# One fixed order of SBUF rooms: where the two operands of each matmul start

## The chip, the cores and the metric

The kernel runs on 1 core of one Trainium2 chip. The metric is device time in microseconds (us) of one execution. The median of three runs of the kernel before is 893.97 us.

## What is computed

Attention with fixed masks feeds two feed-forward layers in float32. `moe` has the gate below, `moe2` has s * relu(h)^2 + b. There are 2304 tokens, 512 model columns and 2048 hidden columns.

```python
scores = np.where(masks, scale * (q @ k.T), -1e9)      # 4 batches, 8 heads, 576 positions of 64
x = softmax(scores) @ v                                # -> 2304 x 512
h = x @ w_in                                           # 512 x 2048
g = np.where(h >= 1, h, np.where(h <= -1, 0, (h + 1) ** 2 / 4))
x = g @ w_out                                          # 2048 x 512
h2 = x @ w2_in
out = (s * np.maximum(h2, 0) ** 2 + b) @ w2_out
```

## The kernel before

Every float32 operand of the two feed-forward layers is held as two parts in the type fp32r, a high part (`xh`, `gh`, plane 0 of a weight) and the rest (`xl`, `gl`, plane 1). A product of two such operands is three TensorE matmuls: high by high, high by rest, rest by high. All of them have the same size: a **standing** operand of 128 partitions by 128 columns, which is loaded into the array, and a **moving** operand of 128 partitions by 256 columns, which is streamed through it. In `nc.tensor.matmul(out, a, b)`, `a` stands and `b` moves. There are 6,696 of these products.

The tokens are cut into 18 blocks g of 256: blocks 0 to 8 belong to the first feed-forward layer (the first half of the kernel, with attention woven into it), blocks 9 to 17 to the second (the second half). The hidden columns are cut into 8 pairs p. `layer1(g, p)` (line 836) does 24 products: the weights of `w_in` stand, `xh` and `xl` move. `layer2` (line 991) does 24 in the first half: the weights of `w_out` stand, the gate's two planes in `g` move. `layer2_fast` (line 904) does 21 in the second half, a seven-product form for a two by two split. There the roles are exchanged: slices of `gh` and `gl` stand and the weights move. `PASSES` says in which order blocks and pairs come, and `LAG` = 2 puts layer 2 of a pair two pairs behind its layer 1.

Between the two, `activate` (line 851) and `combine` (line 879) make the gate and its two parts on ScalarE, VectorE and GpSimd. `w_load`, `w_high`, `w_bits` and `w_parts` bring the weights in (float64 in, two parts out).

All calls go through the recorder `Order`. It notes each operation with its operands, and `issue()` (line 272) works out a start time for each from costs and due times, sorts them, and emits them. A tile is asked of the pool only when the first operation that uses it is emitted, in `real()` (line 161). So SBUF addresses follow the order of first use. Since small tiles (`half`, `narrow`, `mx`, `sm`, `sbt`) fall between the large ones, the large ones start at different places modulo 256 bytes. All slices that a product takes of a tile lie whole multiples of 256 bytes from its start, apart from those that the change moves.

Start addresses modulo 256 of the operands, from the built program:

```text
room                              role                        before                     after
xh, xl (2 + 2 rooms)              move in layer 1             64                         64
w (32 rooms)                      stand in layer 1 and in     32 in 25 rooms, 160 in 4,  128 in all
                                  layer 2 of the first half;  128 in 2, 64 in 1
                                  move in layer2_fast
g (3 rooms)                       move in layer 2             64                         64
gh within g                       stand in layer2_fast        64                         192
gl (3 rooms: raw0, raw1, as)      stand in layer2_fast        160 in 2, 128 in 1         192 in all
```

The distance (start of what stands less start of what moves, modulo 256 bytes) over the 6,696 products is then:

```text
distance       224   96    32    64   128     0   192
before        3888 1020   883   328   266   166   145
after            0    0     0  6689     0     0     7
```

Of the kernel before, what the change touches and what calls it, by code (L numbers as in the profile page):

```python
# [20 lines left out]
P = 128  # L21
# [5 lines left out]
NF = DFF // P  # L27
# [89 lines left out]
    )  # L117


class Order:  # L120


# [30 lines left out]
    def bank(self, pool, choices, name, kind):  # L153


        t = self.tile(pool, [P, 512], F32, f"bank_{kind}", len(self.choices) + 1, name)
        self.choices[t.tensor.name] = choices
        self.uses[t.tensor.name] = []
        return t

    def real(self, x):

        if not isinstance(x, bass.AP) or x.tensor.name not in self.place:
            return x
        (tag, _), pool, shape, dtype, bufs, name = self.place[x.tensor.name]
        if x.tensor.name not in self.tiles:
            if self.in_psum(x):
                tag, bufs = self.taken[x.tensor.name], 1
            self.tiles[x.tensor.name] = pool.tile(shape, dtype, tag=tag, bufs=bufs, name=name)
        t = self.tiles[x.tensor.name]  # L170
        v = bass.AP(tensor=t.tensor, offset=x.offset, ap=[list(d) for d in x.ap])
        return v if x.dtype == dtype else v.bitcast(x.dtype)
# [217 lines left out]
def attention_moe_moe(ctx, tc, q, k, v, w1_in, w1_out, w2_in, w2_out, s_in, b_in, consts, out):  # L390
    nc = Order(tc.nc)
# [4 lines left out]
    ident = nc.tile(sb, [P, P], F32, "ident")  # L396
    narrow = nc.tile(sb, [P, N_CONST], BF16, "narrow")
    mask_l, mask_s, ident_b = narrow[:, :N_MASK_L], narrow[:, N_MASK_L:N_MASK_L + N_MASK_S], narrow[:, N_MASK_L + N_MASK_S:]
    sbt = nc.tile(sb, [P, 2], F32, "sbt")
# [285 lines left out]
    wc = {}  # L685
# [189 lines left out]
    def turn(i, rooms, name):  # L875
        n_room[i] += 1
        return rooms[n_room[i] % len(rooms)](name)

    def combine(g, p, u, h, gt):

        (a21, a11, a22, a12), (h21, h11, h22, h12) = [[x[:, i * P:(i + 1) * P] for i in range(4)] for x in (u, h)]
        s4 = turn(0, (main["qk"][0], main["v"][0]), f"s{g}_{p}")[:, :4 * P]
        s1, s2, s3, s4_ = [s4[:, i * P:(i + 1) * P] for i in range(4)]
        gh = gt.rearrange("p x n -> p (x n)")[:, :7 * P]
        if (g, p) == LAST:
            gl = xs[g, 1][1].rearrange("p x n -> p (x n)")[:, :7 * P]
        else:
            gl = turn(1, (*main["raw"], main["s"]), f"gl{g}_{p}")[:, :7 * P].bitcast(F32R)

        def split(x, c, eng=nc.gpsimd):  # L890
            nc.scalar.activation(out=gh[:, c], in_=x, func=AF.Copy)
            eng.tensor_tensor(out=gl[:, c], in0=x, in1=gh[:, c].bitcast(F32), op=ALU.subtract)

        nc.vector.tensor_tensor(out=s1, in0=h21, in1=a22, op=ALU.add)
        nc.vector.tensor_tensor(out=s2, in0=s1, in1=h11, op=ALU.subtract)
        nc.vector.tensor_tensor(out=s3, in0=h11, in1=a21, op=ALU.subtract)
        nc.vector.tensor_tensor(out=s4_, in0=h12, in1=s2, op=ALU.subtract)
        split(u[:, P:], slice(0, 3 * P))
        split(s4, slice(3 * P, 7 * P), nc.vector if g == LAST[0] and p >= NP - 2 else nc.gpsimd)
        gs[g, p] = gh, gl  # L900
# [48 lines left out]
    def last_two(g, p0, part):  # L949
        y, o = ys.pop(g), [turn(2, (main["qk"][1], main["v"][1]), f"o{g}_{p0}_{i}")[:, :DM] for i in range(2)]  # L950
        (c21, c22), (c11, c12), (p21, p22), (p11, p12), (m1, m6), (m2, m5), (m4, m7), (m3, _) = [
            (x[:, :HM], x[:, HM:]) for x in (*o, part[:, 0], part[:, 1], *y)
        ]
        pairs = [(p, gs.pop((g, p))) for p in (NP - 2, NP - 1)]

        def multiply(n, p, x):
            a, b = PRODUCTS[n]
            o, c, w = y[n // 2][:, n % 2 * HM:(n % 2 + 1) * HM], slice(a * P, a * P + P), wt[1, p][b]
            for i, j in ((0, 0), (0, 1), (1, 0)):
                nc.tensor.matmul(o, x[i][:, c], w[:, j], start=False, stop=p == NP - 1 and i == 1, skip_group_check=True)  # L960

        def leave(i, j, c, queue):
            r0 = (g - NBLK) * N + i * P
            queue.dma_start(out=out[r0:r0 + P, j * HM:(j + 1) * HM], in_=c)

        nc.in_line = True
        for i, n in ((0, 0), (0, 1), (0, 2), (0, 3), (1, 0), (1, 1), (1, 2), (1, 3), (0, 4), (0, 5), (1, 4), (1, 5), (0, 6), (1, 6)):
            multiply(n, *pairs[i])
        nc.in_line = False
        add = dict(op=ALU.add)  # L970
        nc.scalar.activation(out=c11, in_=m1, func=AF.Copy)
        nc.gpsimd.tensor_tensor(out=p11, in0=c11, in1=p11, **add)
        nc.vector.tensor_tensor(out=c21, in0=m6, in1=c11, **add)
        nc.gpsimd.tensor_tensor(out=p21, in0=c21, in1=p21, **add)
        nc.vector.tensor_tensor(out=c22, in0=m5, in1=c21, **add)
        nc.gpsimd.tensor_tensor(out=p22, in0=c22, in1=p22, **add)
        nc.vector.tensor_tensor(out=c11, in0=m2, in1=p11, **add)
        leave(1, 0, c11, nc.sync)
        nc.vector.tensor_tensor(out=p12, in0=c22, in1=p12, **add)
        nc.scalar.activation(out=p11, in_=m7, func=AF.Copy)  # L980
        nc.vector.tensor_tensor(out=p21, in0=m7, in1=p21, **add)
        nc.gpsimd.tensor_tensor(out=c22, in0=p11, in1=p22, **add)
        leave(0, 1, c22, nc.sync)
        nc.vector.tensor_tensor(out=c21, in0=p21, in1=m4, op=ALU.subtract)
        leave(0, 0, c21, nc.scalar)
        nc.vector.tensor_tensor(out=c12, in0=m3, in1=p12, **add)
        leave(1, 1, c12, nc.scalar)
# [36 lines left out]
    half = nc.tile(sb, [P, 1], F32, "half")  # L1024

    def room(tag, width):
# [4 lines left out]
        p=[room("qp0", 5 * P), room("qp1", S)], v=[room("v0", 9 * D), room("v1", 9 * D)],  # L1031
# [64 lines left out]
    with tc.manual_schedule():  # L1096
        nc.now = -100
        nc.sync.dma_start(out=ident, in_=consts[:, N_MASK_L + N_MASK_S:])
        wide = x_room("wide", N_CONST)[:, 0]
        nc.sync.dma_start(out=wide[:, :N_CONST], in_=consts)  # L1100
        nc.gpsimd.memset(half, 0.5)
        nc.vector.tensor_copy(narrow, wide[:, :N_CONST])

        nc.now = -1000
        zeros = nc.tile(sb, [P, 2 * N], F32R, "u", bufs=U_BUFS)
        nc.gpsimd.memset(zeros.bitcast(F32), 0.0)
        idle = nc.bank(ps, ("y1",), "idle", "y")
        nc.tensor.matmul(idle[:, :256], zeros[:, :P], zeros[:, :256], start=True, stop=True)
        nc.fill(idle[:, :256], zeros[:, :P], zeros[:, :256])
        nc.now = -100  # L1110
        for i, t in enumerate(STARTS):
            b, pair = divmod(i, 4)
            plan(Unit(b, FIRST_PAIRS[pair], borrowed(MEMORY[i]) if i in MEMORY else main, i < QUICK, i < NATURAL), t)
        for f in range(NF):
            plan_w(f)
        at(todo[0][0], pump)

        run(-1)
        nc.sync.dma_start(out=sbt[:, 0:1], in_=bass.AP(tensor=s_in.tensor, offset=s_in.offset, ap=[[0, P], [1, 1]]))
        nc.sync.dma_start(out=sbt[:, 1:2], in_=bass.AP(tensor=b_in.tensor, offset=b_in.offset, ap=[[0, P], [1, 1]]))  # L1120
        nc.now = -15
        x_split(0)
        nc.now = -2
        x_split(1)
        slot, behind = 0, []
        for n, (g, p0, p1) in enumerate(PASSES):

            order = []
            for p in range(p0, p1):
                order.append((1, g, p0, p1, p))  # L1130
                behind.append((2, g, p0, p1, p))
                if len(behind) > LAG:
                    order.append(behind.pop(0))
            nxt = PASSES[n + 1][0] if n + 1 < len(PASSES) else g
            if n + 1 == len(PASSES):
                order.insert(-2, order.pop(-2))
            for i, (layer, b, *pp, p) in enumerate(order):
                run(slot)
                if slot == 0:
                    nc.fill()  # L1140
                if layer == 1:
                    activate(b, p, layer1(b, p))
                else:
                    second(b, p, *pp)
                if i == p1 - p0 + 1 and nxt not in xs:
                    x_split(nxt)
                elif i == p1 - p0 + 1 and n + 1 == len(PASSES):
                    part = last_part(g, p0)
                slot += 1
        nc.now += 1  # L1150
        last_two(g, p0, part)
        nc.issue()


# [24 lines left out]
```

## Time and profile before

| | |
|---|---|
| median of 3 runs | 893.97 us (892.34 to 895.43) |
| the profiled execution | 893.28 us |
| its span, first to last instruction | 891.5 us |
| TensorE busy | 873.8 us, 98% of the span |
| VectorE, ScalarE, GpSimd busy | 481.4, 494.6, 422.5 us |
| mean granted TensorE clock | 0.996 |

The span is cut into 40 equal slices on the page. TensorE is busy in nearly all of each, and its clock is granted in full nearly throughout. Matmuls overlap each other in the records: a record is about 0.28 us long, while the next one starts much sooner. So the busy share says little about the pace, and the pace has to be read from start to start.

### The profile page before, as it was taken

To read this page: it belongs to the slowest core of one execution; us is meant where nothing else is said; L and a number is where in the kernel's file an instruction comes from. 1 tells how busy PE (TensorE), PEld (TensorE's weight loads), DVE (VectorE), ACT (ScalarE), POOL (GpSimd) and SP (SyncE) were. 2 spreads that over 40 slices of the span, in tenths; PEclk is the share of its full clock that TensorE was granted. 3 is DMA by queue.
4 is the path that set the end of the run, shared out by engine and by line. 5 is a ranking of instruction groups with operands and counts; after the bars stand their busy time and mean duration, and the time that the engine had idled before them with its cause. 6 is when DMAs were issued, how large, how long until landed. Compare 5 with 4: busy or idle time off the path is not lost.

```text
span 891.5 us, 21976 instructions
## 1 busy us (share of the span) xinstructions
PE 873.8 (98%) x8872; PEld 861.9 (97%) x8872; DVE 481.4 (54%) x994; ACT 494.6 (55%) x1098; POOL 422.5 (47%) x363
## 2 busy tenths in 40 slices
PE   8889999999999999999999999999999999999998
PEld 7789999899999999999999999999999999999998
DVE  3597553434433442333675789645457955444545
ACT  3776775544444442333654587656667655555554
POOL 7376552122122112223464577867744865554554
PEclk9999999999999999999999999999999999999999
DMA  9998323323322221002625732444435233222211
GB/s 177 318 326 257 89 78 89 76 42 76 61 35 65 54 86 48 25 25 83 211 110 193 232 120 97 142 137 137 154 96 189 96 131 103 98 96 96 95 49 48
DMA packets 125535, 103.38 MB, mean 116 GB/s; under 512 B 86689, under 2 KB 103841, under 8 KB 125433
## 3 DMA queue, kind: packets, MB, share of 16 engines
q1 hardware_dynamic: 122008, 100.52, 37.6%
q8 instruction: 70, 1.15, 0.5%
q10 hardware_dynamic: 2656, 0.85, 0.4%
q0 software_dynamic: 768, 0.60, 0.4%
q14 instruction: 33, 0.26, 0.1%
HBM read 73.63 MB, written 28.31 MB: 114 GB/s over the span
## 4 chain that ended last, share of the span: by engine, by line
PE 94%; DMA 2%; DVE 1%; issue 1%; ACT 1%; SPq 0%; POOL 0%; DVEq 0%; ACTq 0%
PE h L386 45%; PE y L386 42%; PE s L386 3%; PE o L386 2%; PE p L386 1%; DMA wr<-in_moe_w_in_dram 1%; PE t L386 1%; DMA mem<-in_q_dram 1%; DVE wc L386 1%; PE idle L386 1%; ACT u L386 0%; DVE u L386 0%; SPq L386 0%; POOL w L386 0%; ACT h L386 0%
## 5 line engine op out<-in xcount | busy, mean ns | idle before, releaser
L386 PE MATMUL h<-xh,w 128*128 128x256 f32 x2304 | 434.7, 281 | 4.4 <-ACT xr L386 2.0
L386 PEld LDWEIGHTS h<-xh,w 128*128 128x128 f32 x2304 | 363.6, 189 | 6.0 <-ACT xr L386 2.1
L386 PE MATMUL h<-xl,w 128*128 128x256 f32 x1152 | 323.1, 281 | 1.0 <-DVE xl L386 1.0
L386 PE MATMUL y<-g,w 128*128 128x256 f32 x1728 | 220.3, 281 | 0.0
L386 PEld LDWEIGHTS h<-xl,w 128*128 128x128 f32 x1152 | 217.4, 189 | 1.4 <-DVE xl L386 1.2
L386 POOL TENSOR_TENSOR g<-u,g 128x512 fp32r<-128x512 f32 x72 | 95.5, 1326 | 246.2 <-ACT g L386 163.7
L386 PEld LDWEIGHTS y<-g,w 128*128 128x128 f32 x1728 | 209.0, 188 | 0.8
L386 PE MATMUL y<-w,g 128*128 128x256 f32 x852 | 155.3, 281 | 0.0
L386 ACT ACTIVATE u<-h 128x512 f32<-128x512 f32 x144 | 85.7, 597 | 105.4 <-PE h L386 65.5
L386 PEld LDWEIGHTS y<-w,g 128*128 128x128 f32 x852 | 130.7, 188 | 0.0
L386 DVE TENSOR_SCALAR u<-h 128x512 f32<-128x512 f32 x72 | 49.6, 688 | 144.0 <-PE h L386 141.8
L386 PE MATMUL y<-w,gl 128*128 128x256 f32 x426 | 118.3, 281 | 0.0
L386 DVE TENSOR_SCALAR h<-h,sbt 128x512 f32<-128x512 f32 x72 | 58.8, 816 | 108.7 <-ACT h L386 108.5
L386 POOL TENSOR_TENSOR gl<-u,g 128x384 fp32r<-128x384 f32 x71 | 74.7, 1052 | 89.0 <-ACT g L386 85.1
L386 ACT ACTIVATE u<-u,half 128x512 f32<-128x512 f32 x72 | 52.0, 722 | 114.9 <-DVE u L386 114.8
L386 POOL TENSOR_TENSOR gl<-s,g 128x512 fp32r<-128x512 f32 x70 | 91.6, 1309 | 40.3 <-ACT g L386 38.4
L386 ACT ACTIVATE g<-u 128x512 fp32r<-128x512 f32 (+1 forms) x143 | 82.5, 578 | 32.3 <-DVE u L386 25.4
L386 POOL TENSOR_TENSOR w<-wc,w 128x512 fp32r<-128x512 f32 x56 | 77.0, 1384 | 35.7 <-ACT w L386 30.5
L386 PEld LDWEIGHTS y<-w,gl 128*128 128x128 f32 x426 | 79.8, 188 | 0.0
L386 DVE TENSOR_TENSOR u<-h,u 128x512 f32<-128x512 f32 x72 | 49.4, 686 | 26.7 <-ACT u L386 26.5
L386 DVE TENSOR_SCALAR wc<-wr 128x512 int32<-128x512 int32 x64 | 47.4, 751 | 17.9 <-POOL w L386 7.8
L386 ACT ACTIVATE g<-s 128x512 fp32r<-128x512 f32 x71 | 44.6, 628 | 20.4 <-DVE s L386 20.3
(111 smaller groups left out, 941.9 us busy)
## 6 DMA issues: line engine op xcount, KB each, us to landing
wr<-in_moe_w_in_dram SPq DMA_DIRECT2D x32, 512.0 KB
wr<-in_moe_w_out_dram SPq DMA_DIRECT2D x32, 512.0 KB
x<-o SPq DMA_DIRECT2D x36, 256.0 KB
scratch<-x SPq DMA_DIRECT2D x18, 512.0 KB
y<-o SPq DMA_DIRECT2D x22, 256.0 KB
scratch<-y SPq DMA_DIRECT2D x11, 512.0 KB
xhd<-xh SPq DMA_DIRECT2D x8, 512.0 KB
xld<-xl SPq DMA_DIRECT2D x8, 512.0 KB
```

The costliest lines, as they stand in the source:

```text
L386: getattr(getattr(self.nc, engine), op)(*args, **kw)
```

## The change

The tiles that are listed in `HOMES` are taken from the pool before anything is emitted, in the order of that list, by a new method `settle`. The list has the small tiles in places where they leave the large ones at the same place modulo 256 bytes. The high part of the gate in `combine` starts 32 elements (128 bytes) into its room instead of at its beginning. The table above gives the addresses that come out. Seven products, of the last pair's `gl`, keep another distance (192).

```diff
+G_SHIFT = 32
+HOMES = (
+    "ident", "u", *(f"w{f}_{x}" for f in range(NF) for x in range(2)), "xr0", "xr1", "v0", "v1", "mx", "sm", "qp0", "qp1", "wc",
+    "half", "sbt", "as", "raw0", "raw1", "narrow", "xh", "xl", "g",
+)
...
+    def settle(self, tags):
+
+        for tag in tags:
+            name = f"{tag}_0"
+            pool, shape, dtype, bufs, title = self.place[name][1:]
+            self.tiles[name] = pool.tile(shape, dtype, tag=tag, bufs=bufs, name=title)
...
-        gh = gt.rearrange("p x n -> p (x n)")[:, :7 * P]
+        gh = gt.rearrange("p x n -> p (x n)")[:, G_SHIFT:G_SHIFT + 7 * P]
...
         last_two(g, p0, part)
+        nc.settle(HOMES)
         nc.issue()
```

`issue()` doesn't look at addresses. Both built programs have 12,098 instructions, in the same order on every engine, with the same sizes and the same waits. Only addresses differ.

## Rows read from the trace of the kernel before

**Rows 1.** The page: busy time of the engines, and granted clock by slice.
```profile
PE 873.8 (98%) x8872; PEld 861.9 (97%) x8872; DVE 481.4 (54%) x994; ACT 494.6 (55%) x1098; POOL 422.5 (47%) x363
...
PEclk9999999999999999999999999999999999999999
```

**Rows 2.** The page: the chain that ended last, by engine.
```profile
PE 94%; DMA 2%; DVE 1%; issue 1%; ACT 1%; SPq 0%; POOL 0%; DVEq 0%; ACTq 0%
```

**Rows 3.** The page, costliest groups: the products of the layers, with counts.
```profile
L386 PE MATMUL h<-xh,w 128*128 128x256 f32 x2304 | 434.7, 281 | 4.4 <-ACT xr L386 2.0
...
L386 PE MATMUL h<-xl,w 128*128 128x256 f32 x1152 | 323.1, 281 | 1.0 <-DVE xl L386 1.0
L386 PE MATMUL y<-g,w 128*128 128x256 f32 x1728 | 220.3, 281 | 0.0
...
L386 PE MATMUL y<-w,g 128*128 128x256 f32 x852 | 155.3, 281 | 0.0
...
L386 PE MATMUL y<-w,gl 128*128 128x256 f32 x426 | 118.3, 281 | 0.0
```

**Rows 4.** Three stretches, all engines: busy us (instructions), clock, DMA share, GB/s.
```profile
400.00:500.00 100.00, 100.00 (x858) 100.00 (x857) 57.58 (x95) 49.12 (x83) 43.73 (x35) 1.00 0.48 159
500.00:600.00 100.00, 100.00 (x850) 100.00 (x849) 72.60 (x157) 68.54 (x128) 76.14 (x61) 1.00 0.39 131
600.00:700.00 100.00, 100.00 (x850) 100.00 (x849) 61.10 (x156) 65.69 (x120) 65.02 (x54) 1.00 0.40 138
```

**Rows 5.** TensorE's waits from 400 us on: us, times, longest.
```profile
PE y L386 <- ACT g L386: 0.8, 1, 0.8
PE h L386 <- DVE s L386: 0.3, 1, 0.3
```

**Rows 6.** Timeline, layer 1, distance 64: start us, us, engine, line, operation.
```profile
477.52 0.28 PE L386 MATMUL h<-xl,w 128*128 128x256 f32 x1
...
478.54 0.28 PE L386 MATMUL h<-xl,w 128*128 128x256 f32 x1
```

**Rows 7.** Timeline, layer 1 of another block, distance 64.
```profile
432.63 0.28 PE L386 MATMUL h<-xl,w 128*128 128x256 f32 x1
...
433.69 0.28 PE L386 MATMUL h<-xl,w 128*128 128x256 f32 x1
```

**Rows 8.** Timeline, layer 1, distance 224, with the start of what follows.
```profile
481.57 0.28 PE L386 MATMUL h<-xh,w 128*128 128x256 f32 x1
...
484.37 0.40 PE L386 MATMUL y<-g,w 128*128 128x256 f32 x2
```

**Rows 9.** Timeline, layer 1, distance 96.
```profile
471.54 0.28 PE L386 MATMUL h<-xl,w 128*128 128x256 f32 x1
...
472.96 0.28 PE L386 MATMUL h<-xl,w 128*128 128x256 f32 x1
```

**Rows 10.** Timeline, one turn of `layer2_fast`, distances 192, 32, 0 and 128.
```profile
821.69 0.40 PE L386 MATMUL y<-halves,g 128*128 128x256 f32 x2
...
824.17 0.28 PE L386 MATMUL h<-xh,w 128*128 128x256 f32 x1
```

**Rows 11.** Timeline, filler products on one room of zeros, distance 0.
```profile
5.74 1.95 PE L386 MATMUL idle<-u 128*128 128x256 f32 x15
```

**Rows 12.** Timeline: first and last unbroken stretch of 12 products at distance 64.
```profile
108.54 0.28 PE L386 MATMUL h<-xl,w 128*128 128x256 f32 x1
...
109.56 0.28 PE L386 MATMUL h<-xl,w 128*128 128x256 f32 x1
...
872.22 0.28 PE L386 MATMUL h<-xl,w 128*128 128x256 f32 x1
...
872.90 0.28 PE L386 MATMUL h<-xl,w 128*128 128x256 f32 x1
```

**Rows 13.** Groups of TensorE, attention's matmuls: first and last of the six costliest.
```profile
L386 PE MATMUL p<-ident,s 128*128 128x128 f32 x66 | 9.6, 274 | 0.0
...
L386 PE MATMUL o<-pt,v 54*64 54x54 f32 x280 | 6.6, 222 | 0.5 <-ACT pt L386 0.5
```

## The prediction

> **What bounds the kernel now.** I read the page first. TensorE is busy for 98% of the span with its clock granted in full, no other engine is busy for more than 55% [rows 1], and the chain that ended last is TensorE for 94% [rows 2]. So either TensorE waits less, or each product takes less time; nothing else can shorten the run. Then the waits: from 400 us on TensorE waits for another engine for 1.1 us in all [rows 5]. The end is set by the number of products times the pace at which they follow each other. The large groups have 2304, 1152, 1728, 852 and 426 products [rows 3]; with the smaller groups of the same shape they are 6,696. The change leaves their number, order, sizes and waits as they are, so only the pace can move.
>
> The pace now is read where only products of the layers run. From 400 to 700 us TensorE starts 858, 850 and 850 matmuls [rows 4], 2,558 in 300 us, which is 117.3 ns for one. I went over the starts of the whole timeline as well: of the 6,696 products 6,558 are followed by another within 135 ns, and the rest stand before a wait, a break or attention's work. These 6,558 are what a new pace would act on.
>
> **Does the pace depend on the distance?** Nothing on the page says so, but before has seven different distances, so the timeline can be asked. I take products of the same kind, all at full clock and without a wait, and read from start to start. An `xl` product comes once in three in layer 1, so two of its rows are a multiple of three products apart.
> - At distance 224, which 3,888 products have, 24 products take 484.37 - 481.57 = 2.80 us, or 116.7 ns [rows 8].
> - At 96 (1,020 products) 12 take 1.42 us, or 118.3 ns [rows 9].
> - In `layer2_fast`, where distances change from product to product, 21 take 2.48 us, or 118.1 ns [rows 10].
> - At 64, the distance that the change gives to all but seven, there are two paces. In one stretch 9 products take 1.02 us, or 113.3 ns [rows 6]; in another 9 take 1.06 us, or 117.8 ns [rows 7].
> - At 0, 15 filler products take 1.95 us with a last record of 0.28 us: 1.67 us for 14, or 119.3 ns [rows 11].
>
> So the pace depends on where the rooms stand, by some per cent, and 64 is the only distance at which a run of layer 1 holds 113.3 ns. At the others the starts alternate around 116 to 120 ns, and a gap of 113 ns comes up only now and then. At 64 a stretch settles in its first five products at most into one pace or the other, and none that I found leaves it again within its twelve products.
>
> Which of the two it settles into isn't told by the address, which is the same each time. There are 17 unbroken stretches of twelve at distance 64, the first from 108.43 us and the last from 871.76 us [rows 12]. Twelve of them settle at 113.3 ns and five at 117.7 ns, and eight of the last nine are of the quick kind. Over the fourth and later products of all stretches, in step or still settling (151 products), the mean is 114.9 ns. That is the value that I take for a kernel in which all products stand at 64.
>
> **The change part by part.** (1) *Pace of layer 1 and of the first half's layer 2.* Both have moving rooms at 64 and standing rooms at 128 then, exactly the pair that rows 6 and 7 show. (2) *Pace of `layer2_fast`.* It has the same distance with other starts, moving at 128 and standing at 192. No row shows this pair. Bounds from the nearest rows: 113.3 ns if only the distance counts and it settles well [rows 6], 119.3 ns if the start counts and it is as bad as the filler [rows 11]. I take the distance as what counts, hence 114.9, since rows 6 to 9 differ in it while the moving rooms all start at 64; the other end stays in the range. (3) *Sum.* 6,558 products by (117.3 - 114.9) ns are 15.7 us. (4) *Crossings.* In the second half the two layers alternate every 24 and 21 products. The last product of each turn is followed by one whose operands stand elsewhere (the next to be loaded stands at 128 or 0 from what moves), and a stretch needs some products to settle. I count 5 ns for each of some 143 crossings, 0.7 us back. Left: 15.0 us. (5) *Shift of `gh` by 128 bytes.* ScalarE and GpSimd write and read the same number of elements in the same order; nothing. If it cost them 1%, they would still be idle for 24% of the busiest stretch, where GpSimd has 76.14 us in 100 [rows 4]. (6) *Attention.* Its operands move to other rooms too, and I can't say to which pace. Its six largest groups of matmuls sum to 50.2 us, from 9.6 down to 6.6 [rows 13]. If they moved as far as the two paces are apart, 3.8%, it would be 1.9 us either way. I take 0. (7) *Taking rooms early.* It is done while the program is built and adds no instruction; nothing.
>
> **What comes late next.** TensorE at 114.9 ns asks for its inputs 2% sooner. GpSimd's 76% of the busiest stretch becomes 78%, and VectorE's 73% becomes 74% [rows 4]; neither becomes the bound. TensorE's waits are 1.1 us after 400 us [rows 5], and I leave them as they are. Breaks in the first 100 us, at transfers and attention's steps, keep their length.
>
> The profiled execution took 893.28 us. 893.28 - 15.0 = 878.3 us. The median of the three runs lies 0.7 us above it, so I predict 879.0 us.
>
> [...] Rows 6 to 9 show the same instruction, at the same clock and with no wait, at four paces, with nothing but the rooms between them. [...] No stretch of this trace keeps a pace below 113.3 ns.
>
> **The rivals.**
> - *Mostly quick.* When every product stands at 64, a quick stretch has nothing to throw it out, so it may last for hundreds of products instead of twelve. At 113.3 ns throughout the gain is 6,558 x 4.0 = 26.2 us: 867.8 us. For it: eight of the last nine stretches. Against: five settled slow, and every crossing draws anew. From four fifths quick on, the time is below 872.
> - *Mostly slow.* The same, with the slow pace as the one that lasts. At 117.7 ns throughout the change costs 0.4 x 6,558 = 2.6 us: 896.6 us; with under three tenths quick it is 889 to 896.6. For it: four of the first nine stretches, in the part with attention, where breaks are frequent. Against: eight of the last nine.
> - *Slower: a worse pace in `layer2_fast`.* If the pair 128 and 192 settles at the filler's 119.3 ns, its 1,507 products that follow each other lose 1.2 ns against their 118.1, or 1.8 us, and with all others slow (5,051 by 0.7 ns, since they average 117.0, or 3.5 us) the kernel ends near 899. It decides once layer 1 is quick for less than a tenth of its products.
> - *The change doesn't do what it says, or addresses don't matter.* The addresses of the built program are as said. If the two paces come from something else that happens to go with these rooms, such as when the stretch starts, the time stays at 894. Little for it, since 224 and 96 hold their patterns wherever they come up.
>
> **How the numbers follow.** A mix of both paces, 872 to 889 us: 0.52, and the forecast. Mostly quick, 867 to 872: 0.25. Mostly slow, 889 to 896.6: 0.15. No effect, 894: 0.02. A worse pace, 897 to 901: 0.06. About 0.3% is what a measurement of this kernel can tell from no change: 891.3 to 896.7. Of the mostly slow cases some 0.05 lie below 891.3. So faster has 0.52 + 0.25 + 0.05 = 0.82, the same 0.10 + 0.02 = 0.12, slower 0.06. The range from 867.0 to 892.0 leaves out some 0.18 above and hardly anything below.
>
> **What would show it.** The count of matmuls between 400 and 700 us rises from 2,558 to some 2,610, and the starts of `xl` rows three products apart are 0.34 us apart for long stretches where 0.35 to 0.36 stood. In a slow stretch 0.353 stands for many turns. In `layer2_fast` 21 products take 2.41 us instead of 2.48. TensorE's waits after 400 us stay near 1 us; if they grow to several us, the gain was handed to a wait. The forecast is wrong if the pace at 64 depends on more than the distance, which the second half would show against the first, or if one pace holds nearly throughout.

## The result, and the profile after

The changed kernel takes 881.34 us (median of four runs, 880.04 to 883.39). The ratio of its time to that of the kernel before is 0.9861, with a 95% interval of 0.9829 to 0.9894. The prediction was 879.0 us in a range of 867 to 892. A fourth run of the kernel before took 4,834.57 us and counts neither in its median nor in the ratio.

The profiled execution took 880.8 us, with a span of 879.0 us; before had 891.5 us. The page after, engines and granted clock by slice, then the chain that ended last; it answers to [rows 1, 2]:

```profile
PE 863.5 (98%) x8872; PEld 851.5 (97%) x8872; DVE 483.9 (55%) x994; ACT 494.2 (56%) x1098; POOL 423.6 (48%) x363
...
PEclk9989999999999999999999999999999999999999
...
PE 94%; DMA 2%; ACT 1%; DVE 1%; issue 1%; SPq 0%; POOLq 0%; POOL 0%; DVEq 0%; ACTq 0%
```

TensorE has the same 8872 instructions, is still busy for 98% and still makes up 94% of the chain. It needs 10.3 us less for them. The costliest groups, to be read beside [rows 3]:

```profile
L400 PE MATMUL h<-xh,w 128*128 128x256 f32 x2304 | 428.7, 280 | 3.4 <-ACT xr L400 2.0
...
L400 PE MATMUL h<-xl,w 128*128 128x256 f32 x1152 | 321.9, 280 | 1.0 <-DVE xl L400 1.0
L400 PE MATMUL y<-g,w 128*128 128x256 f32 x1728 | 216.5, 279 | 0.0
...
L400 PE MATMUL y<-w,g 128*128 128x256 f32 x852 | 154.0, 281 | 0.3 <-DVE o L400 0.3
...
L400 PE MATMUL y<-w,gl 128*128 128x256 f32 x426 | 118.0, 281 | 0.0
```

The mean length of one record hardly moves (281 to 280 ns), because records overlap: a product lasts 0.28 us and the next starts after 0.115 us. What gets shorter is the time from start to start, so the pace has to be read from counts in a fixed stretch. The same three stretches as in [rows 4], all engines:

```profile
400.00:500.00 100.00, 100.00 (x885) 100.00 (x884) 64.88 (x103) 51.86 (x89) 48.53 (x37) 1.00 0.52 169
500.00:600.00 100.00, 99.67 (x861) 99.47 (x860) 71.32 (x157) 69.95 (x129) 77.87 (x64) 1.00 0.39 130
600.00:700.00 100.00, 99.72 (x859) 99.54 (x858) 67.00 (x168) 66.77 (x123) 66.05 (x55) 1.00 0.40 138
```

885, 861 and 859 matmuls start where 858, 850 and 850 did: 2,605 in place of 2,558. The gain isn't spread evenly. The first stretch, which lies in the first half, goes up by 27 and the other two by 11 and 9. TensorE's waits after 400 us stay small, 1.4 us beside the 1.1 us of [rows 5]:

```profile
PE y L400 <- ACT g L400: 0.8, 1, 0.8
PE y L400 <- DVE o L400: 0.3, 1, 0.3
PE h L400 <- DVE s L400: 0.3, 1, 0.3
```

**Where the 12.5 us of span come from.** The mean time from start to start, over all products of the layers that another follows within 135 ns, in ns:

| | first half, layer 1 | first half, layer 2 | second half, layer 1 | `layer2_fast` | all (count) |
|---|---|---|---|---|---|
| before | 116.96 | 116.96 | 117.15 | 118.43 | 117.35 (6,558) |
| after | 114.72 | 114.64 | 114.82 | 117.25 | 115.31 (6,540) |

These means, and others below that no row shows, are worked out from the single starts of the traces. 6,540 products by 2.04 ns are 13.3 us. Products with a longer step after them went from 79 (19.4 us) to 97 (23.9 us). 18 of these are products that were in the class above, worth 2.1 us there, so 2.4 us are new. Everything else got 1.5 us shorter: that is the filler products on `u` in the first 40 us (from 18.1 to 16.6 us), while the steps of attention's matmuls changed by -0.7 to +0.5 us for a group and by less than 0.1 in sum. 13.3 - 2.4 + 1.5 are the 12.5 us but for rounding.

Of the 4.5 us by which these long steps grew, 2.2 lie before 50 us, 1.4 between 150 and 200 us and 0.9 after 550 us. In the first two TensorE's granted clock was lower after: 0.90 in the mean up to 50 us where before had 0.93, and 0.97 from 150 to 200 us where before had 1.00. Two windows of them, before:

```profile
44.00:50.00 6.00, 4.92 (x28) 4.51 (x27) 5.89 (x9) 4.24 (x9) 3.54 (x3) 0.72 0.92 247
...
155.00:165.00 10.00, 8.45 (x164) 7.54 (x163) 3.63 (x6) 3.08 (x7) 0.00 (x0) 1.00 0.26 57
```

and after:

```profile
44.00:50.00 6.00, 5.08 (x24) 5.08 (x24) 5.83 (x9) 4.21 (x9) 3.58 (x3) 0.50 0.94 224
...
155.00:165.00 10.00, 8.45 (x151) 7.29 (x150) 3.65 (x6) 3.09 (x7) 0.00 (x0) 0.83 0.39 79
```

From 155 to 165 us TensorE is busy for the same 8.45 us and has the same two pauses at attention's steps (0.47 and 1.09 us), but behind the second its granted clock is lower after, 0.83 in the mean and not 1.00, and 13 fewer matmuls start. Why the clock fell here in one execution and not in the other isn't settled. It needn't be the change: the mean granted clock of the kernel before lies between 0.989 and 0.998 from one execution to the next, and the two that are compared here have 0.996 and 0.992.

**Two paces, and who gets which.** Three places of the timeline after, TensorE alone (start us, us, engine, line, operation). First the end of attention's last break, after which layer 1 goes on:

```profile
332.07 0.90 PE L400 MATMUL o<-pt,v 54*64 54x54 f32 x44
...
333.59 0.28 PE L400 MATMUL h<-xl,w 128*128 128x256 f32 x1
...
335.97 0.28 PE L400 MATMUL h<-xl,w 128*128 128x256 f32 x1
```

From 333.59 to 335.97 us are 21 products in 2.38 us, 113.3 ns each, the quick pace of [rows 6]. This pace then stays for the rest of the first half, through layer 1 and layer 2 alike. Then one cycle of the second half, from layer 1 to `layer2_fast` and back:

```profile
787.31 0.28 PE L400 MATMUL h<-xl,w 128*128 128x256 f32 x1
...
789.01 0.28 PE L400 MATMUL h<-xl,w 128*128 128x256 f32 x1
...
789.24 0.40 PE L400 MATMUL y<-halves,g 128*128 128x256 f32 x2
...
791.71 0.29 PE L400 MATMUL h<-xh,w 128*128 128x256 f32 x1
```

In layer 1 15 products take 1.70 us, 113.3 ns each. At the entry, before these rows, the step goes through some 121, 122, 116 and 114 ns. The 21 products of `layer2_fast` take 2.47 us, 117.6 ns each: the slow pace of [rows 7], though the distance is 64 here too. The whole second half is like this in the main: of the unbroken turns, 49 of 55 with 24 products of layer 1 settle quick, and 43 of 48 with 21 products of `layer2_fast` settle slow. Most of the others come behind turns that were cut short.

### The profile page after: what moved, and what is told of

The parts are those of the page before. It is cut to its first block, busy times and chain, and to the rows that moved or that the text cites. A ratio compares the mean times of both kernels' runs of the same rounds, so it can differ in the third digit from the quotient of the medians.

```text
span 879.0 us, 21976 instructions
## 1 busy us (share of the span) xinstructions
PE 863.5 (98%) x8872; PEld 851.5 (97%) x8872; DVE 483.9 (55%) x994; ACT 494.2 (56%) x1098; POOL 423.6 (48%) x363
## 4 chain that ended last, share of the span: by engine, by line
PE 94%; DMA 2%; ACT 1%; DVE 1%; issue 1%; SPq 0%; POOLq 0%; POOL 0%; DVEq 0%; ACTq 0%
PE h L400 44%; PE y L400 42%; PE s L400 3%; PE o L400 2%; PE p L400 1%; PE idle L400 1%; PE t L400 1%; DMA raw<-in_q_dram 1%; DMA mem<-in_q_dram 1%; DMA wr<-in_moe_w_out_dram 0%; DVE o L400 0%; ACT u L400 0%; DVE wc L400 0%; ACT xr L400 0%; DVE u L400 0%
## 5 line engine op out<-in xcount | busy, mean ns | idle before, releaser
L400 PE MATMUL h<-xh,w 128*128 128x256 f32 x2304 | 428.7, 280 | 3.4 <-ACT xr L400 2.0
L400 PE MATMUL y<-g,w 128*128 128x256 f32 x1728 | 216.5, 279 | 0.0
L400 PEld LDWEIGHTS y<-g,w 128*128 128x128 f32 x1728 | 205.3, 188 | 0.8
```

The costliest lines, as they stand in the source:

```text
L400: getattr(getattr(self.nc, engine), op)(*args, **kw)
```

## The experiments

In the texts on record, "distance" is as in the prediction: the start of what stands less that of what moves, modulo 256 bytes. A "turn" is an unbroken run of products of one layer, and a cycle is one turn of each. Each ratio is to the kernel before as it ran beside the experiment, with medians of 894.78 to 895.6 us there, so times of different experiments compare to 1 or 2 us at best. A number in `HOMES` stands for a gap: `settle` takes an unnamed room of so many bytes in that place. The kernels named bench hold nothing but runs of the same product, at addresses that are chosen freely (shortened):

```python
def run(n, m, d):            # m: where the moving room starts; d: distance
    s = (m + d) % 256
    for i in range(n):
        nc.tensor.matmul(bk[:, :N], st[d // 16 * 16][:, s // 4:s // 4 + P],
                         mv[:, m // 4:m // 4 + N], start=True, stop=True)
```

### Distance and pace without the kernel around them

> No layer and no attention: only runs of products of the layers' size (128 by 128 standing, 256 moving, fp32r, constant data) on rooms at chosen distances (start of what stands less start of what moves, modulo 256 bytes), and zeros as output. It measures the disputed pace by itself. Runs of 48 at every distance in steps of 16, each entered from 8 products at distance 0; distance 64 at eight starts; distance 64 entered from twelve products at each other distance; alternations of 24 and 21 products as in the second half (moving at 64, then at 128, both at distance 64; and moving at 0, then 64). Theory A (distance, and the step in which a run is entered): at 64 a run holds 113.3 ns or 117.7 ns whatever its start, and which of the two follows from what stood before; all other distances stay at 116 to 120 ns. Theory B (starts): at 64 the pace differs from start to start, quick at a moving start of 64 and slow at 128, whatever stood before. In the alternations A gives 113.3 for the 24 and 117.7 for the 21 in both pairs; B gives the slow pace to the pair at 128 and 192 alone.

Timeline of bench1: runs of 48 products, each run entered from a run at distance 0 (start us, us). The pace is the length less one record of 0.28 us, by 47. `mv` moves and starts at 0 until the last two rows, where it starts at 64 and 128. `ate` is distance 64, `atg` 96, `atm` 192, `ato` 224.

```profile
39.08 5.82 PE L155 MATMUL bank<-mv,ate 128*128 128x256 f32 x48
...
52.36 5.79 PE L155 MATMUL bank<-mv,atg 128*128 128x256 f32 x48
...
92.27 5.61 PE L155 MATMUL bank<-mv,atm 128*128 128x256 f32 x48
...
105.22 5.77 PE L155 MATMUL bank<-mv,ato 128*128 128x256 f32 x48
...
124.92 5.62 PE L155 MATMUL bank<-mv,ate 128*128 128x256 f32 x48
...
137.73 5.61 PE L155 MATMUL bank<-mv,ate 128*128 128x256 f32 x48
```

Distance 64 takes 117.9 ns in the first row (5.54 / 47) and 113.6 and 113.4 in the last two; 192 takes 113.4, 224 takes 116.8 and 96 takes 117.2 by these rows. From the single starts, the settled pace by distance in ns:

```text
distance   0     16    32    48    64            80    96    112
pace     120.0 118.3 118.3 118.3 113.3 | 117.8 118.8 117.4 120.2
distance  128   144   160   176   192           208   224   240
pace     118.6 118.2 119.9 118.0 113.3 | 117.8 116.7 116.6 119.9
```

Only 64 and 192 have the quick pace, and both have a second, slow one (of 192 bench2 shows it). The other distances were run with one start of the moving room, 0, and entered from distance 0. Four bytes to either side of 64 the quick pace is gone: 60 gives 119.8 ns and 68 gives 118.3. At 64, with eight different starts of the moving room, seven runs were quick and one slow. The pair of `layer2_fast` (moving 128, standing 192, last row) is as quick as the pair of layer 1. Then the same pair of rooms (moving 0, standing 64), entered first from distance 0 and then from 16:

```profile
164.78 4.40 PE L155 MATMUL bank<-mv,ate 128*128 128x256 f32 x36
...
170.44 4.25 PE L155 MATMUL bank<-mv,ate 128*128 128x256 f32 x36
```

(4.40 - 0.28) / 35 is 117.7 ns, and (4.25 - 0.28) / 35 is 113.4: the same instruction on the same addresses has both paces. Of 15 entries from other distances into this pair 13 came out quick, and of 10 into the pair of `layer2_fast` seven. So the distance decides which paces are possible, and what ran before picks one of two.

### What picks one of the two paces

> Runs of products alone, as in bench1, zeros as output. Alternations of 24 products (layer 1 of the second half: moving at x, standing at w) and 21 (its layer 2: moving at w, standing at g), five times each, for four choices of x, w, g at distances 64 or 192, each entered in three ways; then 30 products at distance 64 and 192 entered in six ways; then 600 products without a break at distance 64, twice, the second time entered from distance 176, which led to the slow pace in bench1. Theory A (a step that is kept until something breaks it, and the crossing alone chooses the next): with x 64, w 128, g 192 the 24 run at 113.3 and the 21 at 117.7 ns as in bench1; with g at 64, where the next operand to load stands at distance 0 at both crossings, both run at 113.3; the two runs of 600 keep their pace to the end, one quick and one slow. Rival (it drifts): within 600 products a run leaves the slow pace for the quick one or the other way.

Runs of 600 at distance 64, the first entered quick, the second slow, with a short run at 176 between:

```profile
402.47 68.18 PE L155 MATMUL bank<-mv,ate 128*128 128x256 f32 x600
470.49 1.58 PE L155 MATMUL bank<-mv,atl 128*128 128x256 f32 x12
471.90 70.83 PE L155 MATMUL bank<-mv,ate 128*128 128x256 f32 x600
```

(68.18 - 0.28) / 599 is 113.4 ns, and (70.83 - 0.28) / 599 is 117.8. The first has its moving room at 64, the second at 0. Neither drifts towards the other, so a pace is kept until something breaks it. The cycles of this bench show what breaks it. In the following five turns layer 1 (24) is at 64 and layer 2 (21) at 192:

```profile
95.46 2.99 PE L155 MATMUL bank<-mv,ate 128*128 128x256 f32 x24
...
98.29 2.64 PE L155 MATMUL bank<-mv,atm 128*128 128x256 f32 x21
...
100.76 2.90 PE L155 MATMUL bank<-mv,ate 128*128 128x256 f32 x24
...
103.50 2.55 PE L155 MATMUL bank<-mv,atm 128*128 128x256 f32 x21
...
105.88 2.99 PE L155 MATMUL bank<-mv,ate 128*128 128x256 f32 x24
```

2.99 and 2.64 us are slow turns, 2.90 and 2.55 quick ones: slow, slow, quick, quick, slow, without end. The crossing from 64 into 192 keeps the pace, and the one back exchanges it. Theory A, which had both turns at 113.3 ns here, missed. With the pair of the change (64 in both, layer 2 with other rooms) the turns are quick, slow, quick, slow; all three entries began quick. In bench1 a cycle at 64 with other rooms (moving 0, then 64) began slow, and went slow, quick, slow, slow before it settled into the same quick, slow. Of the two other cycles here, one (192, then 64) runs in pairs like the five turns above, and one (192 in both) settles slow in both turns.

### The shift of gh left out

```diff
-G_SHIFT = 32
+G_SHIFT = 0
```

> The change without its shift of the gate's high part: the rooms stay, the high part starts at its room's beginning, so in layer 2 of the second half 1,008 products get distance 192 and 504 keep 64. Theory A (distance and step): these 1,512 products lose the pace of one steady distance, 118.4 ns as before the change instead of 117.3, so 1.7 us more than the change: 883. If the shift were worth nothing, 881; if alternating distances let the step fall into the quick pace now and then, below 881.

It measured 881.64 us, 0.9861 of before (0.9822 to 0.9899): the same as the change, though the interval doesn't exclude the 883 of theory A either. The stretches, as above:

```profile
400.00:500.00 100.00, 100.00 (x885) 100.00 (x884) 60.70 (x99) 51.51 (x87) 46.77 (x35) 1.00 0.51 169
500.00:600.00 100.00, 100.00 (x863) 100.00 (x863) 71.78 (x158) 69.95 (x130) 77.65 (x63) 1.00 0.38 128
```

`layer2_fast` now has distance 192 for two thirds of its products. It is quicker than with the change, 116.27 ns against 117.25, but layer 1 of the second half is slower, 116.00 against 114.82. Turn by turn at the end of the second half (q where the products from the seventh on follow at 113.0 to 114.3 ns, s at 117.2 to 118.3, . elsewhere, here at 119.0; each turn of layer 1 stands above the turn of `layer2_fast` that follows it):

```text
the change   layer 1      qqqqqqqqqqqqqqqqqqqqqqqq
             layer2_fast  ssssssssssssssssssssssss
no shift     layer 1      qsqsqsqsqsqsqsqsqsqsqsqs
             layer2_fast  q.q.q.q.q.q.q.q.q.q.q.q.
```

The two differ by 1.18 ns x 1,726 = 2.0 us in one layer and 0.98 ns x 1,507 = 1.5 us back in the other. So the shift is worth nothing that can be measured; the gain is that of the rooms' order.

### All of `layer2_fast` at 192

Gaps of 128 bytes ahead of `as` and of `xh`, and no shift, so that `gh` and `gl` both stand at 64. Layer 1 stays at 64.

```diff
-G_SHIFT = 32
+G_SHIFT = 0
-    "half", "sbt", "as", "raw0", "raw1", "narrow", "xh", "xl", "g",
+    "half", "sbt", 128, "as", "raw0", "raw1", "narrow", 128, "xh", "xl", "g",
```

> The change, but layer 2 of the second half stands at distance 192 instead of 64: gaps of 128 bytes ahead of the three rooms of the gate's rest and ahead of the moving rooms, and no shift of its high part. All else stays at 64. At both crossings of the second half the next operand to load is then at distance 0 from what moves, where the change has 128 on the way into layer 2. Theory A: layer 2 of the second half settles at 113.3 ns instead of 117.3, 1,507 products by 3.9 ns, 6 us less than the change: 875. If distance 192 has no quick pace in the kernel, or the crossing doesn't choose, 881 or more.

881.31 us, 0.9855 (0.983 to 0.988); no 875. Layer 1 of the second half is at 116.01 ns and `layer2_fast` at 115.98: quick and slow whole cycles alternate, as in bench2. Half of 113.3 and half of 117.7 is 115.5, and the settling at each entry is the rest. The second half stays where it was:

```profile
500.00:600.00 100.00, 99.61 (x860) 99.42 (x859) 72.91 (x159) 70.06 (x129) 78.83 (x65) 1.00 0.38 130
```

### One distance for all products, but another one

All distances at 224: is it that the products agree with each other, or that they are at 64?

```diff
-G_SHIFT = 32
+G_SHIFT = 48
-    "half", "sbt", "as", "raw0", "raw1", "narrow", "xh", "xl", "g",
+    "half", "sbt", 160, "as", "raw0", "raw1", "narrow", 192, "xh", "xl", "g",
```

> The change with gaps of 160 and 192 bytes and a shift of 192 bytes, so that all products but seven are at distance 224, the commonest before, instead of 64. Theory A: the pace is 116.7 ns throughout, 6,550 products by 1.4 ns more than with the change, 9 us: 890. Theory C (any one distance will do, since the gain comes from nothing breaking the step): 881 as with the change.

893.66 us, 0.9987 (0.9968 to 1.0006): no change, and theory C's 881 is out. Theory A's 890 was missed as well, by over 3 us: all products go at 116.97 ns, against 117.35 before and the 116.7 that it counted on, which is half of the miss.

```profile
400.00:500.00 100.00, 100.00 (x859) 100.00 (x859) 55.65 (x91) 47.03 (x80) 43.49 (x33) 1.00 0.46 154
```

One distance for all products gains nothing as such; it has to be one that has the quick pace.

### The same distances with other starts

A gap between `u` and the weights moves all rooms behind it by 192 bytes; all distances stay as in the change.

```diff
-    "ident", "u", *(f"w{f}_{x}" ...
+    "ident", "u", 192, *(f"w{f}_{x}" ...
```

> The change with a gap of 192 bytes ahead of the weights' rooms: all distances stay at 64, all starts move down by 64. Layer 2 of the second half then moves from 64 and stands at 128, the pair that is quick in layer 1 with the change, and layer 1 moves from 0 and stands at 64. Theory A (distance and the step of entry): nothing changes, 881 within 1.5 us, layer 2 of the second half at 117.3 ns. Theory B (starts): layer 2 of the second half at 113.3 ns, 1,506 products by 4 ns, 6 us less: 875, as long as layer 1 keeps its pace.

888.46 us, 0.9927 (0.9909 to 0.9946), 6 us slower than the change by the ratios and 7 by the medians. Both theories missed the time. The second half is as with the change (114.95 and 117.23 ns). The loss is in the first half, at 116.59 and 116.79 ns:

```profile
400.00:500.00 100.00, 100.00 (x851) 100.00 (x850) 53.99 (x89) 47.11 (x79) 44.02 (x34) 1.00 0.47 155
500.00:600.00 100.00, 100.00 (x862) 100.00 (x861) 74.97 (x161) 71.02 (x132) 75.94 (x62) 1.00 0.40 137
```

851 where the change has 885, and 862 where it has 861. Does the start decide? Two more gaps at the same place, of 64 and of 128 bytes:

> As e_starts, with a gap of 64 bytes instead of 192: all distances stay at 64, all starts move up by 64. The question is what put e_starts 7 us behind the change: its first half ran at the slow pace from about 330 us to its end, the change's at the quick one. Theory A (the pace after a break is chosen by the step at which the stretch is entered, and is kept to the end of the first half): two outcomes, 881 with 885 or so matmuls from 400 to 500 us, or 888 with 850, and nothing between; the second half is as with the change (860 matmuls from 500 to 600 us). Theory D (the start decides the pace of a stretch): a third value is as likely as either, and the second half changes too.

> As e_gap64, with a gap of 128 bytes: moving rooms of layer 1 at 192, weights at 0, the gate's standing parts at 64. Theory A: 881 with 885 or so matmuls from 400 to 500 us, or 888 with 850; second half as with the change. Theory D: other values, in the second half too.

886.84 us (0.9904; 0.9875 to 0.9933) and 887.08 us (0.9906; 0.9873 to 0.9939). Both count 852 from 400 to 500 us. By the ratios they are 4 us slower than the change, with intervals that overlap its own; by the counts they belong to the slow layout. Their second halves run as with the change (114.9 and 117.2 to 117.3 ns), which speaks against theory D. Timeline of the kernel with 64 bytes at attention's last break:

```profile
330.37 0.90 PE L403 MATMUL o<-pt,v 54*64 54x54 f32 x44
...
331.89 0.28 PE L403 MATMUL h<-xl,w 128*128 128x256 f32 x1
...
334.36 0.28 PE L403 MATMUL h<-xl,w 128*128 128x256 f32 x1
```

21 products in 2.47 us, 117.6 ns, where the change has 2.38 behind the same 44 matmuls. It then keeps this to the end of the first half, some 170 us later. So one entry is worth about 6 us: 170 us at 117.7 instead of 113.3 ns are 170 x 4.4 / 117.7 = 6.4 us, an estimate. Of four layouts with equal distances one enters quick and three slow. That this goes with the layout and not with chance is borne out by the two kernels above whose first half stands as in the change: the one without the shift counts 885 from 400 to 500 us, and the one with `layer2_fast` at 192

```profile
400.00:500.00 100.00, 100.00 (x884) 100.00 (x884) 62.29 (x101) 51.72 (x88) 47.90 (x37) 1.00 0.51 169
```

Why a layout enters as it does is open. The gaps also move the rooms of attention against `ident`, which stands ahead of them, and that wasn't separated.

### The roles of 64 and 192 exchanged

192 for layer 1 and for layer 2 of the first half, 64 for `layer2_fast`:

```diff
-G_SHIFT = 32
+G_SHIFT = 0
-    "ident", "u", *(f"w{f}_{x}" ...
+    "ident", "u", 192, *(f"w{f}_{x}" ...
-    ... "narrow", "xh", "xl", "g",
+    ... "narrow", 128, "xh", "xl", "g",
```

> The roles of 64 and 192 exchanged: the weights' rooms start at 64, the moving rooms of layer 1 and the gate's at 128, the gate's rest at 128, so layer 1 and the first half's layer 2 are at distance 192 and the second half's layer 2 at 64. Both crossings of the second half have distance 0 again. Theory A: both distances have the quick pace, so the second half runs as in e_192; the first half settles where its breaks throw it, as the starts gave 881 or 888 before: 875 to 883. If only 64 were good, layer 1 would lose its gain, 3,380 products by 2 ns or more, and the time would be above 886.

891.78 us, 0.9966 (0.9949 to 0.9982): a miss. The second half is half quick, half slow (115.96 and 116.05 ns), but the first half is slow nearly throughout, at 117.64 and 117.46 ns.

```profile
400.00:500.00 100.00, 100.00 (x852) 100.00 (x851) 55.38 (x90) 46.42 (x79) 43.67 (x33) 1.00 0.46 153
```

In time this is what the rival named (above 886, only 64 is good). Its reason doesn't hold, since 192 runs at 113.3 ns in bench1, in bench2 and in the kernel with `layer2_fast` at 192. But 192 may be entered quick less often: of six entries each in bench2, four came out quick at 64 and one at 192. This kernel also has the gap of 192 bytes behind `u` of the slow layout above, and the two weren't separated. A distance with a quick pace doesn't bring it by itself: this kernel has hardly a product at another distance and is 9 to 10 us slower than the change.

### Is there a cycle that stays quick

> Runs of products alone, zeros as output, to find a second half in which every crossing keeps the quick pace. Twenty cycles of 24 and 21 products, four times each and entered in two ways, all at distances 64 and 192: layer 1 with the gate's input parts in one row or sorted (high parts at 64, rests at 192, in six orders), layer 2 with its 14 high and 7 rest products sorted, standing at 64 or 192. Theory A, from bench2 (a crossing at distance 0 into 64 exchanges the two paces, one into 192 keeps them, a crossing at 128 out of quick gives slow): cycles with an even number of exchanges keep one pace for good, and a cycle of 14 at 192, 7 at 64 and 24 at 64 has a chance to be quick in more than half of its products; no cycle settles at a third pace. Rival: paces after a crossing vary from turn to turn, and no cycle is quick in more than about half of its products (mean 115.5 ns).

None of the twenty stays quick in both turns. With 24 at 64, then 14 at 192 and 7 at 64, a turn of 14 reads

```profile
16.33 1.75 PE L155 MATMUL bank<-mv,atm 128*128 128x256 f32 x14
...
21.55 1.82 PE L155 MATMUL bank<-mv,atm 128*128 128x256 f32 x14
...
26.76 1.75 PE L155 MATMUL bank<-mv,atm 128*128 128x256 f32 x14
```

quick, slow, quick. The best cycle had a mean of 115.4 ns, and the pair of the change has 115.8 in bench2. Over 72 cycles of 45 products that would be 1.3 us, less than the runs of one kernel scatter, and it wasn't built.

> Runs of products alone, zeros as output: can a small product at a crossing make the next turn quick, at less than it costs? Cycles of 24 and 21 products, six times each, with the second half's rooms of the change (64, 128, 192) and of e_192 (64, 128, 64). At the way into layer 2, or back, the last product is followed by a small one (32, 64 or 128 moving columns, or 32 standing columns), or cut in two (128 and 128, 64 and 192). Without it a cycle takes 45 x 115.7 ns = 5.21 us; quick throughout it would take 5.11 us. Theory A: the small product moves the step of entry, so for some of these sizes both turns are quick, and the cycle is shorter than 5.21 us by what is left of 0.1 us after the small product's 25 to 60 ns. Rival: the extra product costs all that it gives, and no cycle is under 5.20 us.

A small product at a crossing can hold both turns on the quick pace, but it costs what it brings. Layer 1 turns of plain cycles with layer 2 at 192, and of the same cycles with a product of 64 columns put in where layer 2 goes back to layer 1:

```profile
591.05 2.78 PE L155 MATMUL bank<-mv,ate 128*128 128x256 f32 x23
...
596.17 2.87 PE L155 MATMUL bank<-mv,ate 128*128 128x256 f32 x23
...
601.47 2.78 PE L155 MATMUL bank<-mv,ate 128*128 128x256 f32 x23
...
919.00 2.87 PE L155 MATMUL bank<-mv,ate 128*128 128x256 f32 x23
...
924.24 2.87 PE L155 MATMUL bank<-mv,ate 128*128 128x256 f32 x23
```

From start to start a plain cycle takes 5.12 us and 5.30 in turn, 5.21 in the mean. In the last two rows 2.87 us doesn't mean slow: the first step of such a turn, behind the extra product, is 0.20 us long, and (2.87 - 0.28 - 0.20) / 21 is 113.8 ns. With the extra product all turns settle at 113.3 ns, and each cycle takes 5.24, so it costs 0.12 us where 0.025 to 0.06 had been named. Those two figures were the author's estimate before the run; scaled by columns from 113.3 ns for 256, an estimate too, 64 and 128 come to 0.028 and 0.057 us. Two of the 32 forms that were run did this (64 columns, with 128 or 32 standing, on the way back from a layer 2 at 192); no other held both turns quick in every cycle. In bench4 no cycle below 5.20 us lasted, so no kernel was built on these either; none of the versions that ran beats the change beyond the intervals.

## Why the prediction was right, and where not

- **What bounds.** Right. TensorE's 98% and its waits of about 1 us stayed, and only the step from product to product changed.
- **Step 1, layer 1 and the first half's layer 2 at 114.9 ns.** It measured 114.7, 114.6 and 114.8. The value is met, but partly by luck. It was taken as the mean of a mix that is drawn anew at every crossing. In fact the pace is mixed only up to 333 us, then quick without a break for 170 us, and in the second half quick in 49 of 55 full turns of layer 1. Had the one entry at 333 us gone the other way, as in three layouts with the same distances, the sum would have been some 6 us less.
- **Step 2, `layer2_fast` at 114.9.** This is the step that failed. It measured 117.25 ns: 1.2 ns gained on 1,506 products, 1.8 us, where 3.5 ns and 5.3 us were counted. The pair 128 and 192 isn't bad as such (113.3 ns in bench1). What the step had wrong is that layer 2 would draw the same mix as layer 1: in the trace after, 55 of 61 quick turns of layer 1, cut ones included, lead into a slow turn of `layer2_fast` and none into a quick one. 21 products take 2.47 us, not the 2.41 that the prediction named.
- **Step 3, the sum.** 15.7 us were predicted and 13.3 measured: some 11.5 for the 5,034 products outside `layer2_fast` (117.0 to 114.7 ns) and 1.8 for it. The term of `layer2_fast` was too large by 3.5 us, and the others brought 0.9 more than their 10.6 (5,051 by 117.0 - 114.9). These two terms come to 15.9 and not 15.7, since the prediction read 117.3 for 117.35 ns.
- **Step 4, crossings.** The 0.7 us for settling are inside the measured means, since the steps of 121 and 122 ns at an entry lie under 135; no cost beside the mean was left over. The 5 ns for each crossing were the author's estimate, and no row shows them. What was wrong is the rival's phrase that every crossing draws anew: once a cycle of bench2 has settled, a crossing keeps the pace or exchanges it in the same way each time.
- **Step 5, the shift.** Nothing for ScalarE and GpSimd, as said (494.2 and 423.6 us busy against 494.6 and 422.5). The one distance that it gives `layer2_fast`, on which step 2 counts, gained the whole kernel nothing: without the shift it takes the same time.
- **Steps 6 and 7.** Attention's 0 is right in sum, by groups that moved by -0.7 to +0.5 us. The 1.5 us by which the rest is shorter lie in the filler products, which the prediction has no term for; the cause of this wasn't looked into.
- **Breaks keep their length.** Wrong by 2.4 us, mainly in the stretches with the lower granted clock, which varies between executions of one kernel too (a mean of 0.989 to 0.998 for the kernel before). The profiled execution gained 2.5 us less than the 15.0 counted: 2.4 less in step 3, 2.4 in breaks, against 1.5 for the rest and the 0.7 of step 4, but for rounding.
- **The rivals.** Mostly quick is true of a stretch of 170 us and of layer 1, and false of `layer2_fast`. Mostly slow is what the first half does in three of four layouts, and with the roles exchanged it cost all but 3 us of the gain. Neither the worse pace nor no effect came up. Two bounds of the rivals are off by their own sums: four fifths quick give 893.97 - 6,558 x (117.3 - 114.2) ns, or 873.6 us and not 872, and three tenths quick give 888 and not 889. That addresses make no difference doesn't hold for these products: with nothing but the distance different, each run entered from distance 0 and a granted clock of 1.00, they settle at 113.3 ns (192) to 120.2 ns (112) in bench1. What in a product takes longer isn't shown by any run.
- **The sign of being wrong.** The prediction named a second half that differs from the first. It does differ, but by the entry and not by the starts: with the rooms moved by 192 bytes `layer2_fast` has the very pair on which layer 1 is quick with the change (moving 64, standing 128), and it still runs at 117.23 ns.

## What to carry to other kernels

Where TensorE is the bound with products that reload what stands each time, read the step from start to start in the timeline: the length of a record doesn't show it (281 ns before and 280 after, while the mean step went from 117.35 to 115.31 ns). If it differs between rooms of the same shape, the start addresses modulo 256 bytes are worth a look, and the order in which pools are first asked fixes them. Judge such a layout by whole stretches on the chip, since the same distances gave 881 us and 887 to 888 us, and most of this lies in how one long stretch was entered.

## What the runs showed of the hardware

- Products of 128 x 128 by 256 in fp32r, one after the other at a granted clock of 1.00, follow each other in 113.3 to 120.2 ns, by the start addresses of their operands and by what ran before (bench1). Of sixteen distances only 64 and 192 reached 113.3 ns; 60 and 68 are at 119.8 and 118.3.
- At 64 and 192 a run settles into one of two paces, 113.3 or 117.8 ns (bench1, bench2). At 64 each held for 600 products (bench2), and the entry picks which (bench1). What state carries it isn't shown by any run here.
- A product of 64 columns put between two turns made a quick cycle 0.12 us longer (5.24 against 5.12 us, bench4), about the step from one product of 256 columns to the next (0.113 us at the quick pace).
